# Six head pairs of the attention's last product as one unit, with the last 64 keys in four 64x64 tiles

## The chip, the cores and the metric

The kernel runs on one core of one Trainium2 chip. The metric is the device time of one execution in microseconds (us), lower is better. The engines are named as in the profile: PE (TensorE matmuls), PEld (TensorE weight loads), DVE (VectorE), ACT (ScalarE), POOL (GpSimd) and SP (SyncE, which only issues DMAs here).

## The reference

The kernel computes an attention layer that mixes its heads before and after the softmax, and two dense layers behind it. The change lies in the attention alone:

```python
def _attn_ref(q, k, v, w_pre, w_post):           # q, k, v: 4 batches, 12 heads, 448 tokens, 64 wide
    scale = 1.0 / np.sqrt(q.shape[-1])
    scores = scale * np.matmul(q, k.transpose(0, 1, 3, 2))
    scores = np.einsum('bhij,hg->bgij', scores, w_pre)
    scores = scores - np.max(scores, axis=-1, keepdims=True)
    attn = np.exp(scores)
    attn = attn / (np.sum(attn, axis=-1, keepdims=True) + 1e-09)
    attn = np.einsum('bhij,hg->bgij', attn, w_post)
    return np.matmul(attn, v).astype(np.float32)  # "AV" below

def reference(...):
    x = attn_out.transpose(0, 2, 1, 3).reshape(B * S, H * D)
    x = _moe_ref(x=x, **moe_kwargs)               # x @ w_in, softmax-weighted, layer norm, @ w_out
    return _moe2_ref(x=x, **moe2_kwargs)          # relu(x @ w_in)^2 @ w_out
```

## The kernel before, in words

The queries of a batch are cut into chunks of 120, 120, 120 and 88 tokens, 16 chunks in all, numbered c = 0 to 15. A chunk is cut into blocks of up to 10 tokens times 12 heads, and two blocks make a slot: slots s = 0 to 89 follow one another in one loop, and the order in which that loop writes its instructions is the order in which each engine runs them. In one slot the loop writes

- the loads that fall due (K, V, Q, and pieces of the first dense layer's weights), the DMAs of K, V and the weight pieces on POOL's queue, and on SP's queue the DMAs that lay scores out anew for slot s + 5 (`shuffle`);
- `pre(s + 2)`: the head mix before the softmax, on PE, into its own four banks;
- `post_out(s - 1)`: two DVE copies that take the result of the head mix after the softmax out of PSUM;
- `qk`: scores of one pair of heads of a later chunk, on PE, taken out by ACT (six per chunk, so most slots have one, a few have two or none);
- `negmax` on DVE and `expo` on ACT for slot s + 2;
- `av`, where a chunk is complete, taken out of PSUM by ACT;
- `weigh(s + 1)` on POOL: three small instructions that make the matrix w, which `post(s + 1)` multiplies by;
- the work on weight pieces (below), and at the end `post(s)` on PE, which needs w of `weigh(s)`.

`qk`, `av` and `post` take their PSUM from one ring of two buffers of two banks each (`ring()`, L132).

AV of a chunk is 6 pairs of heads times 448 keys. The keys come as three tiles of 128 and a rest of 64. V of the rest lies in a tile with zeros (`load_v`, L176): for one head of a pair its 64 keys stand in partitions 0 to 63 and zeros below, for the other the reverse, so that the rest, too, is a product over 128 partitions. A unit `av(c, a)` handles three pairs: for each, four key tiles times two heads, each head in its own half of the output's partitions. Its 24 products of 128 x 64 by 128 x 120 (or by 88) write one bank, and ACT copies that bank out. A chunk has two units, three slots apart (L544: `end + 1 + 3 * a`).

The 48 weight pieces of the first dense layer (`w1pieces`) run beside this: a DMA loads a piece (POOL's queue, at most 7 pieces ahead), ACT squares it, DVE makes three passes over it, POOL makes two (`flush`: L96 and L97), ACT scales it, and SP stores it. The passes of DVE are handed out one at a time by `filler()`: seven in a slot that has a unit of AV, none elsewhere (L610). At most four pieces are between start and flush (L601). In a slot POOL flushes whatever pieces DVE has finished by then, behind the `weigh` of that slot. Once the last piece is stored, `prep_first` loads and splits the weights of the dense layer (POOL: L441), most of it from slot 80 on.

The lines that the change and the prediction touch: `load_v` L176, `post` L277, `av` L319, `flush` L95, `weigh` L261, `narrow_w1` L385, the slot of AV L544, the limit on pieces L601, the passes handed out L610.

Of the kernel before, what the change touches and what calls it, by code (L numbers as in the profile page):

```python
# [7 lines left out]
F32 = mybir.dt.float32  # L8
# [10 lines left out]
def kernel(  # L19
# [23 lines left out]
    R = 10  # L43
# [133 lines left out]
    def load_v(b, j):  # L177
        if j < NJ:
            t = late_p.tile([JW, H, D], F32, tag=f"v_{j}", name="v", bufs=2)
            nc.gpsimd.dma_start(out=t, in_=v[b, j * JW:(j + 1) * JW].rearrange("j (g d) -> j g d", g=H))  # L180
        else:
            t = late_p.tile([128, 2, G2, D], F32, tag=f"v_{j}", name="v", bufs=2)
            src = v[b, j * JW:S].rearrange("j (e g d) -> e j g d", e=2, g=G2)
            for e in range(2):
                nc.gpsimd.memset(t[64 - 64 * e:128 - 64 * e, e], 0.0)
            for e in range(2):
                nc.gpsimd.dma_start(out=t[64 * e:64 * e + 64, e], in_=src[e])
        vv[b, j] = t

    def qk(c, p, dve=0):  # L190
# [88 lines left out]
    def post(s):  # L279

        ps = ring()
        w = ws.pop(s)
        for b in range(2):
            e = es.pop((s, b))
            for j in range(NJ + 1):
                for x in range(2):
                    for u in range(2):
                        c = x ^ u
                        m = H * size(2 * s + b, u ^ b)
                        o = j * JW + c * 64 if j < NJ else NJ * JW  # L290
                        g0, ng = (0, H) if j < NJ else (c * G2, G2)
                        i0 = (b * NU + j * H) * RH
                        nc.tensor.matmul(  # L293
                            out=ps[64 * c:64 * c + 64, u, i0:i0 + ng * RH],
                            lhsT=e[64 * u:64 * u + m, o:o + 64],
                            rhs=w[64 * u:64 * u + m, b, g0:g0 + ng],
                            start=True,
                            stop=True,
                        )
        pps[s] = ps  # L300
# [15 lines left out]
                m, o = size(2 * s + b, g), oa + RH * g  # L316
                nc.vector.tensor_copy(at[c][:, :, o:o + m], pv[:, b, :, 0:m])

    def av(c, a):  # L319

        ch = chunks[c]
        n = ch["n"]
        if c not in xt:
            xt[c] = late_p.tile([128, HP, 120], F32, tag="xt", name="xt", bufs=2)
        ps = ring()
        for q in range(3):
            p = 3 * a + q
            for j in range(NJ + 1):
                t = vv[ch["b"], j]
                for e in range(2):  # L330
                    g = p + e * HP
                    nc.tensor.matmul(  # L332
                        out=ps[64 * e:64 * e + 64, 0, q * 120:q * 120 + n],
                        lhsT=t[:, g] if j < NJ else t[:, e, p],
                        rhs=at[c][:, j * H + (g if j < NJ else p), 0:n],
                        start=(j == 0),
                        stop=(j == NJ),
                    )

        pv = ps[:, 0, 0:360].rearrange("p (q t) -> p q t", q=3)  # L340
        x = xt[c][:, 3 * a:3 * a + 3]
        if n == 120:
            nc.scalar.copy(
                x.rearrange("p q (u i k) -> p q u k i", u=2, i=R),
                pv.rearrange("p q (u k i) -> p q u k i", u=2, i=R),
            )
        else:
            for u, m in enumerate((ch["n0"], n - ch["n0"])):
                nk = -(-m // R)
                kf = m - (R - 1) * nk  # L350
                for k0, k1, i1 in ((0, kf, R), (kf, nk, R - 1)):
                    if k0 < k1:
                        o, z = u * ch["n0"], k0 * R + u * ch["n0"]
                        nc.scalar.copy(
                            x[:, :, o:o + i1 * nk].rearrange("p q (i k) -> p q k i", k=nk)[:, :, k0:k1],
                            pv[:, :, z:z + (k1 - k0) * i1].rearrange("p q (k i) -> p q k i", i=i1),
                        )
        if a == 1:
            at.pop(c)

    def x_out(c, eng=nc.sync):
        ch = chunks[c]
# [21 lines left out]

    def narrow_w1(i):  # L385
        src, dst, k, o = w1pieces[i]
        sq = raw_p.tile([128, WP], F32, tag="w1sq", name="w1sq", bufs=4)
        t = raw_p.tile([128, WP], F32, tag="w1t", name="w1t", bufs=7)
        for step, _ in enumerate(narrow(w1raw.pop(i), sq, t, nc.gpsimd)):
            if step == 3:  # L390
# [77 lines left out]
        nc.sync.dma_start(out=g_sb, in_=g_ln.rearrange("(k p) -> p k", p=128))  # L468


    wz = raw_p.tile([128, 256], F32, tag="w1sq", name="wz", bufs=4)
    nc.gpsimd.memset(wz, 0.0)
    wz = wz.bitcast(mybir.dt.bfloat16)[:, 0:448]

# [64 lines left out]
    for c, ch in enumerate(chunks):  # L539
# [1 line left out]
            for j in range(NJ + 1):  # L541
                at_slot((ch["first"] + 1) // 2 + (3 if c == 0 else 0) + j, load_v, ch["b"], j)
        end = (ch["first"] + ch["nb"] + 1) // 2
        for a in range(2):  # L544
            at_slot(min(end + 1 + 3 * a, NP), av, c, a)
        at_slot(min(end + 6, NP), x_out, c)
    last_qk = max(s for s, js in jobs.items() for f, a in js if f is qk)
    w1at = []
    kept = 0
# [8 lines left out]
    for s in range(lo_s, NP + 2):  # L558
# [39 lines left out]
                f(*a)  # L598
        if 0 <= s + 1 < NP:
            weigh(s + 1)  # L600
        while begun < len(w1at) and w1at[begun] <= s - 3 and len(fill) + len(w1f) < 4:  # L601
            start_w1(begun)
            begun += 1
        for i in scales:
            scale_w1(i)
        for i in sorted(w1f):
            sq, t = w1f.pop(i)
            flush(sq, t)
            w1s[i] = t
        for _ in range(7 if any(f is av for f, a in js) else 0):  # L610
            filler()
        if 0 <= s < NP:
            post(s)
# [421 lines left out]
```

## Time and profile before

| what | us |
|---|---|
| median of the runs shown (lowest to highest of 3) | 1128.45 (1126.77 to 1129.98) |
| the profiled execution: its time, its span | 1130.63, 1128.8 |
| PE busy, share of the span | 1068.8, 95% |
| DVE, ACT, POOL busy | 680.3 (60%), 468.3 (41%), 417.8 (37%) |
| AV's matmuls (L332): busy, first and last start | 82.2, from 56.8 to 411.1 |

The attention fills the first 411 us or so; behind it the dense layers keep PE busy without gaps. The shares over the whole span hide what happens in the attention, where POOL, DVE and ACT carry far more than on the average. A matmul of this kernel is in fp32, and stands in the trace as two PE matmuls and two weight loads: "x48" of L332 is one unit of 24 products.

### The profile page before, as it was taken

What the parts mean: (1) busy time and instruction counts of PE and PEld (TensorE: products, weight loads), DVE (VectorE), ACT (ScalarE), POOL (GpSimd) and SP (SyncE); (2) the same over time, 40 slices, a digit from 0 to 9 for tenths busy, and PEclk for the clock granted to TensorE, in tenths of its full rate; (3) what the DMA queues carried; (4) which work ended last, traced back from release to release, by engine and by line L of the source; (5) the groups of instructions that cost most, each with busy time, mean ns of one, the idle gap of its engine ahead of it and who ended that gap; (6) DMA issues with size and microseconds to landing.
All of it is one profiled execution on the core that took longest, in us unless ns stands there. A gap on an engine that the chain in (4) does not pass through costs nothing.

```text
span 1128.8 us, 30803 instructions
## 1 busy us (share of the span) xinstructions
PE 1068.8 (95%) x12920; PEld 925.7 (82%) x12920; DVE 680.3 (60%) x1201; ACT 468.3 (41%) x1026; POOL 417.8 (37%) x642
## 2 busy tenths in 40 slices
PE   7798987987999899999999999999999999999998
PEld 2464654655656688989989999999999999999998
DVE  2555875765785638534434686366666666766734
ACT  4465765665876624221212466322222322323211
POOL 2464897787694837201110553011111111111100
PEclk9898999998999999999999999999999999999999
DMA  5786778778776624111110654011211121111113
GB/s 154 193 217 208 215 240 248 208 229 232 217 222 189 186 86 127 50 49 57 35 36 21 197 182 124 24 57 56 57 57 56 43 60 53 57 56 56 30 71 126
DMA packets 96715, 135.00 MB, mean 120 GB/s; under 512 B 21728, under 2 KB 81376, under 8 KB 96576
## 3 DMA queue, kind: packets, MB, share of 16 engines
q1 hardware_dynamic: 88640, 110.16, 32.5%
q0 software_dynamic: 6336, 22.22, 6.9%
q8 instruction: 102, 1.67, 0.6%
q10 hardware_dynamic: 1600, 0.64, 0.2%
q14 instruction: 37, 0.30, 0.1%
HBM read 71.65 MB, written 22.81 MB: 84 GB/s over the span
## 4 chain that ended last, share of the span: by engine, by line
PE 86%; issue 4%; POOL 3%; DMA 3%; ACT 2%; DVE 1%; SPq 1%; POOLq 0%; ACTq 0%; DVEq 0%
PE ps_h L899 21%; PE ps_y L938 21%; PE ps_o L745 10%; PE ps_h L453 10%; PE ps_ring L293 7%; PE ps_ring L332 6%; PE ps_pre L236 5%; PE ps_ring L202 5%; DMA sdst<-ssrc 2%; PE ps_tr L731 1%; ACT ssrc L209 1%; POOL sm L265 1%; ACT e L254 1%; POOL w1sq L96 0%; POOL w1t L97 0%
## 5 line engine op out<-in xcount | busy, mean ns | idle before, releaser
L899 PE MATMUL ps_h<-x,ti 128*128 128x384 f32 (+1 forms) x1440 | 241.6, 325 | 0.0
L938 PE MATMUL ps_y<-to,g 128*128 128x384 f32 x1332 | 240.0, 337 | 0.0
L899 PEld LDWEIGHTS ps_h<-x,ti 128*128 128x128 f32 x1440 | 236.5, 188 | 0.0
L938 PEld LDWEIGHTS ps_y<-to,g 128*128 128x128 f32 x1332 | 232.2, 188 | 1.7 <-DVE y L949 1.7
L293 PEld LDWEIGHTS ps_ring<-w,e 60*64 60x64 f32 (+1 forms) x5760 | 105.0, 140 | 75.8 <-issue 46.2
L312 DVE COPY at<-ps_ring 128x420 f32<-128x420 f32 x156 | 87.8, 611 | 110.5 <-PE ps_ring L293 110.5
L293 PE MATMUL ps_ring<-w,e 60*64 60x60 f32 (+2 forms) x5760 | 113.3, 225 | 34.6 <-issue 26.6
L209 ACT COPY ssrc<-ps_ring 128x896 f32<-128x896 f32 x93 | 83.3, 906 | 111.7 <-PE ps_ring L202 99.9
L907 ACT ACTIVATE r<-ps_h 128x384 f32<-128x384 f32 (+1 forms) x80 | 37.5, 469 | 215.7 <-PE ps_h L899 215.7
L453 PE MATMUL ps_h<-w1i,xs 128*128 128x512 f32 x504 | 122.1, 400 | 0.0
L745 PE MATMUL ps_o<-zt,w1o 128*128 128x384 f32 (+1 forms) x720 | 119.9, 326 | 0.0
L254 ACT ACTIVATE e<-ps_pre,nm 128x448 f32<-128x448 f32 x180 | 113.0, 638 | 16.0 <-DVE nm L247 13.3
L908 DVE SCALAR_TENSOR_TENSOR r<-ps_h,r 128x384 f32<-128x384 f32 (+1 forms) x80 | 42.4, 531 | 123.7 <-ACT r L907 123.7
L745 PEld LDWEIGHTS ps_o<-zt,w1o 128*128 128x128 f32 x720 | 116.8, 189 | 0.0
L453 PEld LDWEIGHTS ps_h<-w1i,xs 128*128 128x128 f32 x504 | 95.5, 191 | 21.8
L949 DVE TENSOR_TENSOR y<-ps_y,y 128x768 f32<-128x768 f32 x97 | 92.4, 953 | 31.5 <-PE ps_y L938 31.5
L855 POOL TENSOR_TENSOR ti<-wt,ti 128x384 fp32r<-128x384 f32 x32 | 35.1, 1095 | 205.8 <-ACT ti L854 205.8
L247 DVE TENSOR_REDUCE nm<-ps_pre 128x1 f32<-128x448 f32 x180 | 103.3, 612 | 13.1 <-PE ps_pre L236 12.8
L202 PE MATMUL ps_ring<-k,q 64*64 64x448 f32 x768 | 102.2, 563 | 6.0 <-issue 2.1
L236 PE MATMUL ps_pre<-sdst,wpre_bd 64*64 64x448 f32 x720 | 101.0, 578 | 6.3 <-DMA sdst<-ssrc 3.9
L332 PEld LDWEIGHTS ps_ring<-at,v 128*64 128x64 f32 x1536 | 75.1, 138 | 29.8 <-PE ps_pre L236 12.7
L332 PE MATMUL ps_ring<-at,v 128*64 128x120 f32 (+1 forms) x1536 | 82.2, 263 | 7.5 <-issue 5.4
(84 smaller groups left out, 1183.0 us busy)
## 6 DMA issues: line engine op xcount, KB each, us to landing
sdst<-ssrc SPq DMA_DIRECT2D x172, 210.0 KB
wr<-in_moe_w_in_dram SPq DMA_DIRECT2D x32, 384.0 KB
wr<-in_moe_w_out_dram SPq DMA_DIRECT2D x32, 384.0 KB
w1raw<-in_moe_w_in_dram POOLq DMA_DIRECT2D x24, 256.0 KB, 5.9
w1raw<-in_moe_w_out_dram POOLq DMA_DIRECT2D x24, 256.0 KB, 5.1
out_dram<-y SPq DMA_DIRECT2D x13, 384.0 KB
v<-in_v_dram POOLq DMA_DIRECT2D x12, 384.0 KB, 6.3
xraw<-xD SPq DMA_DIRECT2D x12, 384.0 KB
```

Source lines behind the costliest of these rows:

```text
L202: nc.tensor.matmul(out=ps[64 * u:64 * u + 64, e, 0:S], lhsT=qq[c][64 * e:64 * e + 64, p * n + u * half:p * n + u * half + 64], rhs=k[64 * ...
L209: (nc.vector.tensor_copy if dve else nc.scalar.copy)(ssrc[c][:, p:H:HP, :], ps[:, :, 0:S])
L236: nc.tensor.matmul(out=ps[b][64 * u:64 * u + 64, 0:S], lhsT=wpre_bd[64 * r:64 * r + m], rhs=ds[b][64 * r:64 * r + m], start=True, stop=True,)
L247: nc.vector.tensor_reduce(out=nm, in_=pres[s][b][:, 0:S], op=ALU.max, axis=AX.X, negate=True)
L254: nc.scalar.activation(out=e, in_=pres[s][b][:, 0:S], func=AF.Exp, bias=nms.pop((s, b)), scale=1.0, accum_out=sms[s][:, b:b + 1])
L293: nc.tensor.matmul(out=ps[64 * c:64 * c + 64, u, i0:i0 + ng * RH], lhsT=e[64 * u:64 * u + m, o:o + 64], rhs=w[64 * u:64 * u + m, b, g0:g0 ...
L332: nc.tensor.matmul(out=ps[64 * e:64 * e + 64, 0, q * 120:q * 120 + n], lhsT=t[:, g] if j < NJ else t[:, e, p], rhs=at[c][:, j * H + (g if ...
L453: nc.tensor.matmul(out=ps[:, u], lhsT=t[:, a, cc], rhs=w1i[cc][:, w, u * 512:(u + 1) * 512], start=(cc == 0 and a == 0 and w == 0), stop=( ...
L745: nc.tensor.matmul(out=ps[:, 0:width], lhsT=w1o[k][:, w, cc * 128:(cc + 1) * 128], rhs=zT[:, a, k, 0:width], start=(k == 0 and i == 0), st ...
L899: nc.tensor.matmul(out=ps[:, 0:n], lhsT=ti[:, w, cc, f * 128:(f + 1) * 128], rhs=x2[q][:, a, cc], start=(cc == 0 and i == 0), stop=(cc == ...
L938: nc.tensor.matmul(out=ps[:, u - us[0], 0:DM // 2], lhsT=g[:, a, f, o:o + 128], rhs=to[:, w, f, u * (DM // 2):(u + 1) * (DM // 2)], start= ...
L949: nc.vector.tensor_tensor(out=yo, in0=po, in1=yo, op=ALU.add)
```

## The change

A chunk's AV becomes one unit, `av(c)`, in the slot of the former first half. It uses both banks of one ring buffer: three pairs in each. First come the 36 products over the three full key tiles, then the rest: its V lies in half the space, without zeros, one half of the heads in partitions 0 to 63 and the other half in 64 to 127, and each of the 12 products is 64 x 64 by 64 x 120. Four consecutive ones use four different quarters of the array. `post` writes the last 64 keys of the heads into the partition halves that fit this (the moving operand takes two groups of three heads instead of six in a row). ACT takes the two banks out one after the other. `x_out` comes three slots earlier.

The handing out of the weight pieces changes with it: twelve DVE passes in a slot with AV, one in every odd slot without; up to six pieces between start and flush, with six buffers for the squares instead of four.

```diff
@@ load_v
-            t = late_p.tile([128, 2, G2, D], F32, tag=f"v_{j}", name="v", bufs=2)
-            src = v[b, j * JW:S].rearrange("j (e g d) -> e j g d", e=2, g=G2)
-            for e in range(2):
-                nc.gpsimd.memset(t[64 - 64 * e:128 - 64 * e, e], 0.0)
-            for e in range(2):
-                nc.gpsimd.dma_start(out=t[64 * e:64 * e + 64, e], in_=src[e])
+            t = late_p.tile([128, G2, D], F32, tag=f"v_{j}", name="v", bufs=2)
+            src = v[b, j * JW:S].rearrange("j (a n d) -> j a n d", a=4, d=D)
+            nc.gpsimd.dma_start(out=t[0:64].rearrange("j (a n) d -> j a n d", a=2), in_=src[:, 0:4:3])
+            nc.gpsimd.dma_start(out=t[64:128].rearrange("j (a n) d -> j a n d", a=2), in_=src[:, 1:3])
@@ post
+                        wb = w[64 * u:64 * u + m, b]
+                        if j == NJ:
+                            wb = wb.rearrange("p (a n) i -> p a n i", a=4)
+                            wb = wb[:, 1:3] if c else wb[:, 0:4:3]
...
-                            rhs=w[64 * u:64 * u + m, b, g0:g0 + ng],
+                            rhs=wb,
@@ av
-    def av(c, a):
+    def av(c):
...
+        def product(p, e, half, j):
+            t = vv[ch["b"], j]
+            a, q = divmod(p, 3)
+            rows = slice(0, 128) if half is None else slice(64 * half, 64 * half + 64)
+            g = p + e * HP if half is None else (p + 3 * half) % HP
+            nc.tensor.matmul(
+                out=ps[64 * e:64 * e + 64, a, q * 120:q * 120 + n],
+                lhsT=t[rows, g],
+                rhs=at[c][rows, j * H + g, 0:n],
+                start=(j == 0 and q == 0),
+                stop=(j == NJ and q == 2),
+            )
+
+        for p in range(HP):
+            for j in range(NJ):
+                for e in range(2):
+                    product(p, e, None, j)
         for q in range(3):
...
+            for a in range(2):
                 for e in range(2):
...
+                    product(3 * a + q, e, a ^ e, NJ)
+
+        for a in range(2):
+            pv = ps[:, a, 0:360].rearrange("p (q t) -> p q t", q=3)
...
@@ narrow_w1
-        sq = raw_p.tile([128, WP], F32, tag="w1sq", name="w1sq", bufs=4)
+        sq = raw_p.tile([128, WP], F32, tag="w1sq", name="w1sq", bufs=6)
@@ the slots
-        for a in range(2):
-            at_slot(min(end + 1 + 3 * a, NP), av, c, a)
-        at_slot(min(end + 6, NP), x_out, c)
+        at_slot(min(end + 1, NP), av, c)
+        at_slot(min(end + 3, NP), x_out, c)
@@ the loop over slots
-        while begun < len(w1at) and w1at[begun] <= s - 3 and len(fill) + len(w1f) < 4:
+        while begun < len(w1at) and w1at[begun] <= s - 3 and len(fill) + len(w1f) < 6:
...
-        for _ in range(7 if any(f is av for f, a in js) else 0):
+        for _ in range(12 if any(f is av for f, a in js) else s % 2):
             filler()
```

PE around the AV of chunk 10, slots 64 to 67: L332 is a unit of AV, L293 `post`, L236 `pre`, L202 `qk`. Before, from the first unit to the second:

```order
L332 MATMUL ps_ring<-at,v 64x120 x24
L293 MATMUL ps_ring<-w,e 64x60 x12
...
L202 MATMUL ps_ring<-k,q 64x448 x4
L293 MATMUL ps_ring<-w,e 64x60 x12
...
L202 MATMUL ps_ring<-k,q 64x448 x4
L293 MATMUL ps_ring<-w,e 64x60 x12
...
L202 MATMUL ps_ring<-k,q 64x448 x4
L332 MATMUL ps_ring<-at,v 64x120 x24
```

The same place now (L333 is AV, L295 `post`, L200 `qk`):

```order
L333 MATMUL ps_ring<-at,v 64x120 x48
L295 MATMUL ps_ring<-w,e 64x60 x12
...
L200 MATMUL ps_ring<-k,q 64x448 x4
L295 MATMUL ps_ring<-w,e 64x60 x12
...
L200 MATMUL ps_ring<-k,q 64x448 x4
L295 MATMUL ps_ring<-w,e 64x60 x12
...
L200 MATMUL ps_ring<-k,q 64x448 x4
L295 MATMUL ps_ring<-w,e 64x60 x12
```

The second unit has moved in front, into the first, and the slot three later has no AV.

POOL at the same place: L267 ends `weigh(66)`, L96 and L97 flush a piece, L264 begins `weigh(67)`. Before:

```order
L267 TENSOR_TENSOR w<-wpost_bd,sm 128x120
L96 TENSOR_SCALAR w1sq<-w1sq 128x256
L97 TENSOR_TENSOR w1t<-w1t,w1sq 128x256
L96 TENSOR_SCALAR w1sq<-w1sq 128x256
L97 TENSOR_TENSOR w1t<-w1t,w1sq 128x256
L96 TENSOR_SCALAR w1sq<-w1sq 128x256
L97 TENSOR_TENSOR w1t<-w1t,w1sq 128x256
L264 TENSOR_SCALAR sm<-sm 128x2
```

Now (L265 ends `weigh(66)`, L262 begins `weigh(67)`):

```order
L265 TENSOR_TENSOR w<-wpost_bd,sm 128x120
L96 TENSOR_SCALAR w1sq<-w1sq 128x256
L97 TENSOR_TENSOR w1t<-w1t,w1sq 128x256
L96 TENSOR_SCALAR w1sq<-w1sq 128x256
L97 TENSOR_TENSOR w1t<-w1t,w1sq 128x256
L96 TENSOR_SCALAR w1sq<-w1sq 128x256
L97 TENSOR_TENSOR w1t<-w1t,w1sq 128x256
L96 TENSOR_SCALAR w1sq<-w1sq 128x256
L97 TENSOR_TENSOR w1t<-w1t,w1sq 128x256
L262 TENSOR_SCALAR sm<-sm 128x2
```

Four pieces are flushed between the two `weigh`, where there were three. From chunk 2 to chunk 11 every slot behind an AV now flushes four pieces in a row; before, a slot behind a unit flushed two or three, and there were twice as many such slots.

## Rows read from the trace of the kernel before

**Rows 1.** The page: busy time by engine, and the chain that ended last.
```profile
PE 1068.8 (95%) x12920; PEld 925.7 (82%) x12920; DVE 680.3 (60%) x1201; ACT 468.3 (41%) x1026; POOL 417.8 (37%) x642
PE 86%; issue 4%; POOL 3%; DMA 3%; ACT 2%; DVE 1%; SPq 1%; POOLq 0%; ACTq 0%; DVEq 0%
```

**Rows 2.** Windows: stretch, length, busy time (instructions) by engine, PEclk, DMA share, GB/s.
```profile
110.00:343.00 233.00, 205.83 (x5458) 139.93 (x5454) 167.83 (x367) 157.94 (x378) 186.53 (x333) 0.97 0.76 225
```

**Rows 3.** Timeline of PE: start, us, line, operation, count, idle before.
```profile
305.72 0.96 PE L202 MATMUL ps_ring<-k,q 64*64 64x448 f32 x8
306.61 2.68 PE L332 MATMUL ps_ring<-at,v 128*64 128x120 f32 x48
309.22 1.13 PE L293 MATMUL ps_ring<-w,e 60*64 60x60 f32 x64
310.18 0.96 PE L236 MATMUL ps_pre<-sdst,wpre_bd 64*64 64x448 f32 x8
310.96 0.93 PE L202 MATMUL ps_ring<-k,q 64*64 64x448 f32 x8
311.71 1.11 PE L293 MATMUL ps_ring<-w,e 60*64 60x60 f32 x64
314.15 1.12 PE L293 MATMUL ps_ring<-w,e 60*64 60x60 f32 x64
```

**Rows 4.** Timeline of POOL, the same stretch.
```profile
309.83 0.40 POOL L264 TENSOR_SCALAR sm<-sm 128x2 f32<-128x2 f32 x1 [1.19 <-ACT e L254]
311.58 0.86 POOL L96 TENSOR_SCALAR w1sq<-w1sq 128x256 f32<-128x256 f32 x1
312.52 0.73 POOL L97 TENSOR_TENSOR w1t<-w1t,w1sq 128x256 f32<-128x256 f32 x1
...
316.01 0.73 POOL L97 TENSOR_TENSOR w1t<-w1t,w1sq 128x256 f32<-128x256 f32 x1
316.82 0.22 POOL L264 TENSOR_SCALAR sm<-sm 128x2 f32<-128x2 f32 x1
317.92 0.56 POOL L267 TENSOR_TENSOR w<-wpost_bd,sm 128x120 f32<-128x120 f32 x1
```

**Rows 5.** The chain in order of time, end of the attention: start, us, what.
```profile
395.41 1.13 PE ps_ring L293 x64
405.08 6.25 PE ps_ring L332 x144
411.33 2.96 PE ps_h L453 x12
```

**Rows 6.** Groups of instructions: busy us, mean ns of one, idle before.
```profile
L343 ACT COPY xt<-ps_ring 128x360 f32<-128x360 f32 x24 | 19.8, 823 | 20.8 <-PE ps_ring L332 20.8
L354 ACT COPY xt<-ps_ring 128x150 f32<-128x150 f32 (+2 forms) x24 | 5.3, 376 | 4.1 <-PE ps_ring L332 4.1
L87 DVE SCALAR_TENSOR_TENSOR w1t<-w1raw,w1t 128x256 uint32<-128x256 uint32 x48 | 21.9, 457 | 1.4
L83 DVE SCALAR_TENSOR_TENSOR w1t<-w1raw,w1t 128x256 uint32<-128x256 uint32 x48 | 20.6, 430 | 1.4
L79 DVE TENSOR_SCALAR w1t<-w1raw 128x256 uint32<-128x256 uint32 x48 | 14.7, 306 | 0.1
L382 POOL DMA_DIRECT2D w1raw<-in_moe_w_out_dram x24 | 14.2, 594 | 6.6 <-DVE w1t L79 6.5
```

**Rows 7.** Waits in 110 to 343: who for whom, us, times, longest us.
```profile
PE ps_ring L293 <- issue: 16.6, 12, 3.0
PE ps_ring L332 <- issue: 3.4, 2, 1.8
PE ps_ring L202 <- issue: 2.1, 2, 1.5
PE ps_ring L293 <- POOL w L267: 2.0, 3, 1.1
```

**Rows 8.** A gap of PE on its timeline, and the window behind it.
```profile
194.63 0.71 PE L293 MATMUL ps_ring<-w,e 60*64 60x30 f32 x34 [2.56 <-issue]
195.50:198.90 3.40, 3.40 (x24) 1.62 (x18) 3.22 (x8) 0.62 (x1) 0.40 (x1) 0.50 0.34 113
```

**Rows 9.** Window near the end of the attention, columns as in rows 2.
```profile
392.00:397.00 5.00, 2.10 (x102) 1.91 (x95) 1.54 (x3) 3.53 (x9) 4.75 (x7) 0.99 0.57 160
```

More of the change, by code (lines that the diff above doesn't have):

```diff
@@ L290, in post @@
                         o = j * JW + c * 64 if j < NJ else NJ * JW
-                        g0, ng = (0, H) if j < NJ else (c * G2, G2)
                         i0 = (b * NU + j * H) * RH
+                        ng = H if j < NJ else G2
+                        wb = w[64 * u:64 * u + m, b]
+                        if j == NJ:
+                            wb = wb.rearrange("p (a n) i -> p a n i", a=4)
+                            wb = wb[:, 1:3] if c else wb[:, 0:4:3]
                         nc.tensor.matmul(
@@ L317, in post_out @@
                 nc.vector.tensor_copy(at[c][:, :, o:o + m], pv[:, b, :, 0:m])
-    def av(c, a):
+    def av(c):
         ch = chunks[c]
         n = ch["n"]
-        if c not in xt:
-            xt[c] = late_p.tile([128, HP, 120], F32, tag="xt", name="xt", bufs=2)
+        xt[c] = late_p.tile([128, HP, 120], F32, tag="xt", name="xt", bufs=2)
         ps = ring()
+        def product(p, e, half, j):
[14 more added lines that the diff above has]
+                    product(p, e, None, j)
@@ L326, in av @@
         for q in range(3):
-            p = 3 * a + q
-            for j in range(NJ + 1):
-                t = vv[ch["b"], j]
+            for a in range(2):
                 for e in range(2):
[L331 to L347, printed above, removed]
+                    product(3 * a + q, e, a ^ e, NJ)
+        for a in range(2):
+            pv = ps[:, a, 0:360].rearrange("p (q t) -> p q t", q=3)
+            x = xt[c][:, 3 * a:3 * a + 3]
+            if n == 120:
+                nc.scalar.copy(
+                    x.rearrange("p q (u i k) -> p q u k i", u=2, i=R),
+                    pv.rearrange("p q (u k i) -> p q u k i", u=2, i=R),
+                )
+                continue
@@ L357, in av @@
                         )
-        if a == 1:
-            at.pop(c)
+        at.pop(c)
     def x_out(c, eng=nc.sync):
@@ L468, in load_const @@
         nc.sync.dma_start(out=g_sb, in_=g_ln.rearrange("(k p) -> p k", p=128))
-    wz = raw_p.tile([128, 256], F32, tag="w1sq", name="wz", bufs=4)
+    wz = raw_p.tile([128, 256], F32, tag="w1sq", name="wz", bufs=6)
     nc.gpsimd.memset(wz, 0.0)
```

## The prediction

> **What bounds the kernel now.** I read the page's shares and chain first [rows 1]: PE is busy 95% of the span and carries 86% of the chain, so over the whole it looks like a kernel that only PE bounds. The windows say otherwise for the attention [rows 2]: from 110 to 343 us, where the weight pieces run beside it, PE is busy 205.8 of 233 us, but POOL 186.5 (80%), and DVE 167.8 (72%). The timeline shows the beat there [rows 3]: from one `post` to the next 2.49 us (309.22 to 311.71) and 2.44 us in slots with one qk, PE without a gap; a slot with a unit of AV takes 2.7 more. POOL's timeline of the same stretch [rows 4] shows the other bound: it waits for the exponentials until 309.83, makes w for slot 66, flushes three pieces from 311.58 to 316.82, and only then begins w for slot 67. The waits [rows 7] tell what PE loses in that stage: 16.6 + 3.4 + 2.1 = 22.1 us to "issue" (its instructions were late), and so far only 2.0 us to POOL.
>
> **The change part by part.** *Products.* A unit's 24 products take 2.68 us [rows 3]; the two heads of a pair run side by side in the two column halves, so 12 steps of 0.223 us. The new unit has 18 such steps, 4.02 us, and 12 products of a quarter of the array. If four of them run together, that is three steps; the trace has no such step of 120 columns. Its bounds: qk runs four quarters at 448 columns in 0.75 us (310.96 to 311.71), so 120 columns take at least 0.20; and if they only pair up, six steps of 0.223, 1.34 in all. I take 0.22 a step, near qk's row, which has the same tiles: 0.66. Unit 4.68 us against 5.36: 0.68 less. The 88-wide chunks: the last 144 matmuls, 6.25 us [rows 5], are one unit of 120 and two of 88, so (6.25 - 2.68) / 2 = 1.785 each; new 2.68 + 3 x 0.16 = 3.16 against 3.57: 0.41 less. Twelve chunks and four: 12 x 0.68 + 4 x 0.41 = 9.8 us of PE's time (ends 0 and 10.7).
>
> That the quarters do run together rests on pre: it issues its four quarters in the new unit's pattern, two neighbours in different row halves writing the two partition halves of one bank, and takes 0.78 us (310.18 to 310.96), as long as qk, whose row halves have a bank each [rows 3]. The Trainium skill, "TensorEngine Tiling (Array Packing)", section "Gotcha 1: PSUM Pressure", says that different row tiles cannot access the same PSUM bank at once. By that rule the first and second product of each four would wait for each other and the gain of 9.8 would fall to about 0; by pre's row it stays. The trace disagrees with the rule here; it is a rival below.
>
> *Taking the unit out.* Two copies of 0.82 us follow AV instead of one [rows 6], 1.65. The ring buffer is wanted again by the next slot's qk, post and pre later: 0.96 + 0.78 = 1.74 us [rows 3]. Hidden. In 88-wide chunks six copies of 0.376, 2.26 us: 0.5 late in four chunks, if not hidden 2.0; I take 0.5 in all.
>
> *DVE.* A piece is 0.31 + 0.43 + 0.46 = 1.2 us of DVE [rows 6]. Twelve passes are 4.8 us, beside an AV of 4.68; seven were 2.8 beside 2.68. The odd single pass (0.4) lies in DVE's idle time of 28%. I cost both at nothing; if the cover failed, post's copies would come 0.1 to 0.4 us later in some slots. The memsets that go from POOL are two for each batch, the split DMA issues stay four: nothing.
>
> *POOL.* This is the wait that I expect to be late next. A flush takes (316.82 - 311.58) / 3 = 1.75 us a piece, and four in a row 7.0. Take chunk 10, whose order is shown, with times of rows 3 and 4. AV would end at 306.61 + 4.68 = 311.29, and `post` of slots 64, 65, 66, 67 be ready to start about 311.2, 313.7, 316.15 and 318.6. POOL begins to flush at 311.58 as now, ends at 318.6, and has w for slot 67 1.6 us later: 320.2. PE waits 1.6 us. Before, slot 67 held the second unit, so its `post` was not wanted before about 320.3: that unit was POOL's cover, and it has gone to the front. Behind the waiting `post` PE has the whole next slot queued (pre, qk), and DVE's and ACT's copies wait for those; SP's shuffles run five slots ahead and don't care. The other nine flushes of four differ by the DMA issues that POOL has to make before that `weigh` (0 to 3 of 0.59 us [rows 6]), by 1.5 us less AV in 88-wide chunks, and by 0.75 where one of the three slots has two qk or none. Counted so, place by place (chunks 2 to 11): 2.7, 4.0, 2.6, 0.3, 2.4, 4.0, 3.5, 0, 1.6, 2.8, together 23.9 us if PE lost nothing else. But PE loses 22.1 us to "issue" in about 53 slots [rows 7], 0.42 a slot, 1.25 in the three slots in question, and that time hides as much of POOL's. Left: 1.45, 2.75, 1.35, 0, 1.15, 2.75, 2.25, 0, 0.35, 1.55 = 13.6 us. Ends: 0 and 23.9. POOL's 2.0 us of now [rows 7] are of this kind and go.
>
> *Clock.* A long gap of PE has a price behind it: after one of 2.56 us the granted clock was 0.50, 1.2 GHz, for 3.4 us, in which PE does half the work [rows 8]; 1.7 us lost. I take three of the eight gaps: 5 us. Ends: 0 and 8 x 1.7 = 13.6.
>
> *The end.* The last stretch before the dense layer is AV of 6.25 us [rows 5]; it becomes one 88-wide unit, 3.16, since chunk 14's second half goes to slot 87. There PE idles (busy 2.10 of 5 us, POOL 4.75 [rows 9]), so this is a gain of 3.1, while the faster products of chunks 13 and 14 gain nothing beside POOL. Against the 0.68 + 0.68 + 0.41 counted above that is 1.3 more. The pieces end three slots sooner, and the first split of POOL's next job moves out of this POOL-bound end: I take 1.0 (ends 0 and 1.8).
>
> *Sum.* -9.8 - 1.3 - 1.0 - 2.0 + 0.5 + 13.6 + 5 = +5.0 us against the profiled execution, whose span is 1128.8 and time 1130.63. That execution lies 2.2 above the median, so the time I predict is 1128.45 + 5 = 1133 us.
>
> **The rivals.** *A: POOL's burst stays hidden, faster.* PE's gain comes through: -9.8 - 1.3 - 1.0 - 2.0 = -14.1, 1114 us; with a third of the waits, 1119. For it: three flushes in a row cost PE only 2.0 us so far [rows 7], and late instructions may fall just where POOL would have been late. Against it: the worked example has no slack left. It decides if w comes earlier than 1.25 us after PE wants it in most of the ten places. *B: the waits show in full and each gap is followed by half clock.* -14.1 + 23.9 + 13.6 + 0.5 = +23.9, 1152 us. For it: 80% load of POOL, with bursts; against it: PE's own losses always cover some. *C: the bank rule holds and the quarters run in pairs.* The unit costs as before, so +5.0 + 9.8 = +14.8, 1143 us. Against it: pre's row. *D: the change moves where PE's late instructions fall;* those 22.1 us come in about a dozen and a half gaps, and a few more or fewer make 5 us either way.
>
> **How the numbers follow.** Forecast, from about -1 to +12 around 1133: 0.40 (of it faster 0.04, same 0.14, slower 0.22). A 0.32 (faster 0.28, same 0.04). B 0.16 and C 0.04, slower. D around no change, 0.08 (0.03, 0.02, 0.03). A measurement of this kernel tells about 0.3%, 3.4 us, from no change. Faster 0.35, same 0.20, slower 0.45. The range of 8 in 10 takes in A's 1114 and stops short of B's end: 1114 to 1147. The forecast's own range is 1127 to 1140.
>
> **What would show it.** The step of `post` after an AV slot stays 2.49, the AV unit itself reads about 4.7 us (5.4 would be C). In the slot three behind an AV, `post` has an idle of 1 to 3 us put down to POOL's w in most of chunks 2 to 11, and the waits of PE on POOL rise from 2.0 to some 14 us in that stage. POOL shows eight flush instructions in a row without a gap. The end of the attention has 3 us less AV. I am wrong if those idles are missing (then A), or if PE's "issue" waits change by more than the POOL waits do (then D).

## The result

Over 20 runs of each the changed kernel takes 1133.93 us in the median (1126.11 to 1143.56), the kernel before 1128.41 (1118.31 to 1138.25). The ratio is 1.0057, 95% interval 1.0035 to 1.0079: slower by 0.57%. The profiled execution of the changed kernel took 1140.57 us, 6.6 above its median, that of before 2.2 above its own; so the two traces differ by 9.9 us where the medians differ by 5.5, and what the traces show is larger than what is to be explained.

### The profile page after: what moved, and what is told of

Same layout as the page of the kernel before. It is cut to its first block, busy times and chain, and to the rows that moved or that the text cites. A ratio compares the mean times of both kernels' runs of the same rounds, so it can differ in the third digit from the quotient of the medians.

```text
span 1138.8 us, 30832 instructions
## 1 busy us (share of the span) xinstructions
PE 1064.3 (93%) x12920; PEld 922.3 (81%) x12920; DVE 680.5 (60%) x1201; ACT 467.1 (41%) x1026; POOL 415.1 (36%) x634
## 4 chain that ended last, share of the span: by engine, by line
PE 82%; POOL 7%; DMA 4%; issue 3%; ACT 2%; SPq 1%; DVE 0%; POOLq 0%; ACTq 0%; DVEq 0%
PE ps_h L908 21%; PE ps_y L947 21%; PE ps_h L463 10%; PE ps_o L754 10%; PE ps_ring L295 5%; PE ps_pre L234 5%; PE ps_ring L200 4%; PE ps_ring L333 4%; DMA sdst<-ssrc 3%; POOL w1sq L96 2%; POOL w1t L97 2%; ACT ssrc L207 1%; POOL sm L263 1%; PE ps_tr L740 1%; SPq L214 1%
## 5 line engine op out<-in xcount | busy, mean ns | idle before, releaser
L295 PEld LDWEIGHTS ps_ring<-w,e 60*64 60x64 f32 (+1 forms) x5760 | 108.5, 141 | 85.7 <-POOL w L265 39.0
L295 PE MATMUL ps_ring<-w,e 60*64 60x60 f32 (+2 forms) x5760 | 113.2, 225 | 41.2 <-POOL w L265 23.3
L234 PE MATMUL ps_pre<-sdst,wpre_bd 64*64 64x448 f32 x720 | 105.2, 597 | 11.1 <-issue 7.4
L200 PE MATMUL ps_ring<-k,q 64*64 64x448 f32 x768 | 103.2, 570 | 5.9 <-ACT ssrc L207 2.4
L333 PEld LDWEIGHTS ps_ring<-at,v 128*64 128x64 f32 (+1 forms) x1536 | 69.6, 142 | 25.2 <-ACT ssrc L207 16.2
L333 PE MATMUL ps_ring<-at,v 128*64 128x120 f32 (+3 forms) x1536 | 75.6, 271 | 10.8 <-ACT ssrc L207 10.3
```

Source lines behind the costliest of these rows:

```text
L200: nc.tensor.matmul(out=ps[64 * u:64 * u + 64, e, 0:S], lhsT=qq[c][64 * e:64 * e + 64, p * n + u * half:p * n + u * half + 64], rhs=k[64 * ...
L234: nc.tensor.matmul(out=ps[b][64 * u:64 * u + 64, 0:S], lhsT=wpre_bd[64 * r:64 * r + m], rhs=ds[b][64 * r:64 * r + m], start=True, stop=True,)
L295: nc.tensor.matmul(out=ps[64 * c:64 * c + 64, u, i0:i0 + ng * RH], lhsT=e[64 * u:64 * u + m, o:o + 64], rhs=wb, start=True, stop=True,)
L333: nc.tensor.matmul(out=ps[64 * e:64 * e + 64, a, q * 120:q * 120 + n], lhsT=t[rows, g], rhs=at[c][rows, j * H + g, 0:n], start=(j == 0 and ...
```

## The profile after

The page, answering to [rows 1]: the chain gives PE 4 points less and POOL 4 points more.

```profile
PE 1064.3 (93%) x12920; PEld 922.3 (81%) x12920; DVE 680.5 (60%) x1201; ACT 467.1 (41%) x1026; POOL 415.1 (36%) x634
PE 82%; POOL 7%; DMA 4%; issue 3%; ACT 2%; SPq 1%; DVE 0%; POOLq 0%; ACTq 0%; DVEq 0%
```

Nearly all of the loss lies in one stretch, from the first `post` to that of slot 81, the last before the tail of the attention (1.2 us more pass ahead of it). Its window in the kernel before, columns as in [rows 2]:

```profile
26.00:372.65 346.65, 301.83 (x7808) 204.20 (x7800) 230.36 (x489) 222.47 (x526) 245.11 (x448) 0.96 0.75 217
```

and in the changed kernel, with the stretch of [rows 2] behind it:

```profile
27.24:386.83 359.59, 300.26 (x7850) 204.86 (x7852) 229.90 (x489) 221.70 (x527) 244.26 (x443) 0.93 0.73 211
110.00:343.00 233.00, 192.09 (x4976) 129.69 (x4972) 158.85 (x348) 143.90 (x347) 179.09 (x313) 0.93 0.76 221
```

The stretch is 12.9 us longer: PE is busy 1.6 us less and idle 14.5 us more, and its granted clock fell from 0.96 to 0.93. What follows is shorter: from slot 81 to the dense layer 38.6 us before and 34.6 now. The timeline of PE, around slots 19 to 22 and at slots 36, 58 and the last AV, shows the things that the prediction spoke of:

```profile
104.33 4.69 PE L333 MATMUL ps_ring<-at,v 128*64 128x120 f32 x96
...
111.45 1.08 PE L295 MATMUL ps_ring<-w,e 60*64 60x60 f32 x64
...
113.89 1.10 PE L295 MATMUL ps_ring<-w,e 60*64 60x60 f32 x64
...
119.54 1.93 PE L295 MATMUL ps_ring<-w,e 60*64 60x60 f32 x64 [3.00 <-POOL w L265]
121.27 1.75 PE L234 MATMUL ps_pre<-sdst,wpre_bd 64*64 64x448 f32 x8
...
180.50 0.90 PE L234 MATMUL ps_pre<-sdst,wpre_bd 60*64 60x448 f32 x1 [3.95 <-issue]
...
280.26 1.82 PE L200 MATMUL ps_ring<-k,q 64*64 64x448 f32 x16
286.70 6.13 PE L333 MATMUL ps_ring<-at,v 128*64 128x120 f32 x96 [4.62 <-ACT ssrc L207]
...
417.94 3.57 PE L333 MATMUL ps_ring<-at,v 128*64 128x88 f32 x96
421.43 3.92 PE L463 MATMUL ps_h<-w1i,xs 128*128 128x512 f32 x16
```

The new unit reads 4.69 us, two units of 2.68 before [rows 3]. `post` follows `post` by 2.44 us. In the third slot behind the AV it waits 3.00 us for w, and `pre` and `post` then take nearly twice their time. POOL's timeline of that place, answering to [rows 4], has eight flush instructions in a row between w for slot 21 and w for slot 22, the third behind the AV:

```profile
109.18 0.59 POOL L265 TENSOR_TENSOR w<-wpost_bd,sm 128x120 f32<-128x120 f32 x1
109.85 0.86 POOL L96 TENSOR_SCALAR w1sq<-w1sq 128x256 f32<-128x256 f32 x1
110.79 0.73 POOL L97 TENSOR_TENSOR w1t<-w1t,w1sq 128x256 f32<-128x256 f32 x1
...
115.09 0.90 POOL L96 TENSOR_SCALAR w1sq<-w1sq 128x256 f32<-128x256 f32 x1
116.08 0.73 POOL L97 TENSOR_TENSOR w1t<-w1t,w1sq 128x256 f32<-128x256 f32 x1
116.75 1.17 POOL L392 DMA_DIRECT2D w1raw<-in_moe_w_in_dram  x2
118.00 0.22 POOL L262 TENSOR_SCALAR sm<-sm 128x2 f32<-128x2 f32 x1
118.30 0.72 POOL L263 TENSOR_TENSOR sm<-sm,eps_sb 128x2 f32<-128x2 f32 x1
119.10 0.39 POOL L265 TENSOR_TENSOR w<-wpost_bd,sm 128x120 f32<-128x120 f32 x1
```

The window behind that wait has the granted clock at its lower level (0.50, 1.2 GHz) for 6.83 us; the second window, behind the wait at 286.70, for 3.41:

```profile
119.05:125.88 6.83, 6.34 (x144) 4.46 (x148) 3.71 (x9) 1.99 (x6) 6.13 (x13) 0.50 0.86 277
286.30:289.71 3.41, 3.00 (x30) 3.01 (x32) 0.00 (x0) 2.40 (x6) 0.83 (x2) 0.50 0.65 227
```

The waits of PE in the long stretch, the largest of the changed kernel:

```profile
PE ps_ring L295 <- POOL w L265: 17.2, 8, 3.8
PE ps_ring L295 <- issue: 14.3, 12, 4.3
PE ps_ring L333 <- ACT ssrc L207: 10.3, 6, 4.6
PE ps_pre L234 <- issue: 7.4, 3, 3.9
...
ACT ssrc L207 <- DMA sdst<-ssrc: 18.8, 5, 4.7
```

and the same lines of the kernel before:

```profile
PE ps_ring L293 <- issue: 26.6, 19, 4.3
PE ps_ring L332 <- issue: 5.4, 3, 2.0
...
PE ps_ring L332 <- ACT ssrc L209: 2.1, 5, 0.9
PE ps_ring L293 <- POOL w L267: 2.0, 3, 1.1
...
ACT ssrc L209 <- DMA sdst<-ssrc: 9.0, 3, 4.6
```

PE's waits on POOL rose from 2.0 to 17.6 us here. In the window of [rows 7], from 110 to 343, they rose from 2.0 to 15.6, where some 14 were forecast; their main line there:

```profile
PE ps_ring L295 <- POOL w L265: 15.2, 6, 3.8
```

A second wait, not forecast, rose by 8: AV waits for ScalarE's copy of a QK into `ssrc`. The rows at 280.26 and 286.70 show how. In a slot with two QKs the AV needs the ring buffer of the first; ScalarE copies that buffer only when the shuffles of the chunk two earlier have left `ssrc`, and here they are late. What SP, which issues them, does at this place:

```profile
269.87 4.31 SPq L418 DMA_DIRECT2D w1oD<-w1t  x4
274.27 1.20 SPq L174 DMA_DIRECT2D q<-in_qT_dram  x2
275.56 12.59 SPq L214 DMA_DIRECT2D sdst<-ssrc  x10
```

Ten shuffles stand behind weight stores and take 1.26 us each, in slots that want two every 2.49 us; the median shuffle of the long stretch holds SP for 0.83 us, single ones in this row for up to 2.3. ScalarE's copy starts at 285.75 after waiting 4.68 us for them.

A third line moved that was not to move: "issue", time for which the profile shows no wait, 35.1 us of PE in the stretch before and 24.2 now. The DMA part of the page shows, before and after alike, the transfers that load instructions (number, MB, share):

```profile
q8 instruction: 102, 1.67, 0.6%
```

That is one transfer of 16384 bytes for every 253 of PE's 25840 matmuls and weight loads. Of the 42 gaps put down to "issue" in the two stretches, 41 end 2.2 to 3.0 us after the start of such a transfer, the one at 180.50 in slot 36 for example 2.4 us after. In the 14 traces of this document it is 276 of 284, though the times that lie so far behind a transfer make up only 14% of the stretch. So these gaps are, as far as traces can tell, PE waiting for its own instructions. No run here changes how they are loaded.

## The experiments

A table first, since the same reading recurs: the ratio to before, and from the trace of each the idle time of PE from the first `post` to that of slot 81 (the waits summed by the engine that ended them; small ones left out), with ScalarE's wait for shuffles in the same stretch. The traces are single executions: they lie between 6.8 us below the median of their kernel (e1) and 6.6 above it (changed; e8 6.2 above), so a difference of a few us between two of them is weak evidence. In e3 11.9 us put down to DVE stand in no column.

```
kernel                         ratio   95%               PE idle  POOL  ACT   issue  ACT for shuffles
before                         1                          44.7     2.0   6.1  35.1    9.0
changed                        1.0057  1.0035 to 1.0079   58.8    17.6  16.0  24.2   18.8
e1 one flush a slot            1.0052  1.0019 to 1.0086   57.3    12.7  18.5  21.6   29.5
e2 x stored two slots later    1.0124  1.0086 to 1.0163   67.8    12.6  15.3  38.2   29.0
e3 both                        1.0117  1.0070 to 1.0165   67.3     4.5  22.0  27.1   26.9
e4 one unit, old rest          1.0087  1.0052 to 1.0123   57.8    15.6  11.0  30.6   22.8
e5 no flush, changed           1.0146  1.0109 to 1.0182   63.4     0.7  27.2  34.1   30.2
e6 no flush, before            1.0029  1.0000 to 1.0057   42.9     0.7   9.5  29.9   12.9
e7 AV one slot later           1.0122  1.0091 to 1.0153   50.7    17.6  12.5  17.5   18.3
e8 shorter weigh               1.0064  1.0032 to 1.0097   63.2     7.5  20.8  33.8   37.3
e9 stores on ScalarE's queue   1.0112  1.0067 to 1.0158   60.7     5.9  29.8  23.4   30.0
e10 the same, before           1.0145  1.0096 to 1.0194   57.4     1.9  17.3  36.7   16.4
e11 no flush and e9            1.0121  1.0083 to 1.0158    66.6   1.5  39.8   23.9   30.7
e12 double QKs at the end      1.0033  1.0007 to 1.0059   53.5     8.2  13.9  28.4   18.4
```

The first theory was the prediction's: the burst of flushes costs what the products gain (theory 1). Its rival, from the trace after: SP's order, with the store of x waiting for ScalarE at end + 3, makes the shuffles late (theory 2).

**One flush a slot (e1).**

```
-        for i in sorted(w1f):
+        for i in sorted(w1f)[:1]:
```

> The changed kernel, but POOL flushes at most one weight piece in a slot, so the four that DVE finishes behind an AV are spread over four slots; all else, AV included, stays. Theory 1 (POOL's burst of four flushes, 7 us, holds up w for the slot three behind an AV, whose cover of 2.7 us of AV has gone): the waits of PE's post on POOL's w between 110 and 350 us fall from 16.6 us to under 5, and the time from 1134 to about 1120 us, 0.5 to 1.2% under the kernel before. Rival, theory 2 (the shuffles on SP's queue come late, because the store of AV's result now waits for a longer AV, and the scores' buffer comes free late, so that AV waits for ACT and ACT for a DMA): the waits of PE on POOL may fall, but the AV's waits on ACT (10.3 us) stay, and the time stays at 1130 to 1135.

Ratio 1.0052: nothing came back. PE's longest wait on w fell from 3.8 to 1.7 us, but there are 11 in place of 8, 12.7 us in all, and ScalarE's wait for the shuffles rose to 29.5. The profiled execution was one of the faster, 1131.16 against a median of 1137.99, so its trace shows this kernel at its better.

**The store of x two slots later (e2), and both (e3).**

```
-        at_slot(min(end + 3, NP), x_out, c)
+        at_slot(min(end + 5, NP), x_out, c)
```

> The changed kernel, but the store of a chunk's AV result stands two slots later in SP's queue; all else stays. Theory 2: SP's idle of 2 to 6 us before each such store goes, the shuffles behind it come sooner, the waits of AV on ACT's copy of the scores fall from 10.3 us to about 3, and the time falls by 4 to 8 us, to 1126 to 1130. Theory 1: SP's idles go, but nothing on PE's path changes but a little; 1131 to 1135 us, and the waits of post on POOL's w stay at 14 to 19 us.

> Both edits together: one flush a slot, and the store two slots later. If both waits are on PE's path and apart, the two gains add: 1112 to 1120 us, about 1% under the kernel before. By theory 1 alone it is as the first edit alone (about 1120), by theory 2 alone as the second alone (1126 to 1130).

Both came out the other way, 1.0124 and 1.0117. SP's waits at the store of x did go (40.4 us in the changed kernel, 0.9 in e2, summed over line 376), but those at the weight stores rose from 37.7 to 54.5 and ScalarE's for the shuffles from 18.8 to 29.0. Theory 2 in this form fell: the store of x is not what makes the shuffles late.

**One unit with the old rest (e4).** The last 64 keys again in 128 rows with zero halves, everything else as in the changed kernel.

```
-        for q in range(3):
-            for a in range(2):
-                for e in range(2):
-                    product(3 * a + q, e, a ^ e, NJ)
+            for j in range(NJ + 1):
+                ...
+                        lhsT=t[:, g] if j < NJ else t[:, e, p],
+                        rhs=at[c][:, j * H + (g if j < NJ else p), 0:n],
```

> The changed kernel with the last 64 keys as before: V with zeros and products over 128 partitions, so the AV unit has 48 products in 24 steps, 5.36 us instead of 4.6; the one unit, its slot, the handing out of passes and the flushes stay as changed. Theory 1: 0.7 us more of AV in each chunk is 0.7 us more cover for the burst, so the waits on POOL's w fall by some 5 us while AV's own time rises by 10; 1135 to 1140 us, 0.6 to 1.1% over the kernel before. A rival that the quarter products are what slows the kernel (bank conflicts, more semaphore waits): the time falls to 1128 or under.

Its unit, on its timeline:

```profile
104.55 5.14 PE L333 MATMUL ps_ring<-at,v 128*64 128x120 f32 x96
109.62 0.57 PE L294 MATMUL ps_ring<-w,e 60*64 60x60 f32 x24
```

From the unit's start to `post` that is 5.07 us, against 104.33 to 108.83, 4.51 (the trace's next row), with the quarter tiles and 2 x 2.61 before. With the 88-wide chunks (3.79, 3.39 and 2 x 1.97) the quarters take 12 x 0.56 + 4 x 0.40 = 8.3 us off PE; the ratio to before moved by 0.0030, 3.4 us, with overlapping intervals. So the quarter tiles are not what slows the kernel, the rival of this run. One unit in one slot with the old products is slower than before by 0.9%, and that is shown; but the new handing out of the weight pieces (twelve passes, six pieces) is in this kernel too, and no run takes the two apart.

**No flush (e5 of the changed kernel, e6 of the kernel before).** The two instructions of the flush are left out, so small weights are not set to zero.

```
         for i in sorted(w1f):
             sq, t = w1f.pop(i)
-            flush(sq, t)
             w1s[i] = t
```

> The changed kernel without GpSimd's flush of the narrowed weight pieces (lines 96 and 97 of the changed kernel: small values are not set to zero; 2 instructions and some 1.65 us of GpSimd for each of 48 pieces). Everything else stays, the six pieces in flight and the conversion bursts too. Theory 1 (the burst of flushes behind an AV slot holds the weighting back, and PE with it): PE's waits on w fall from 17 us to under 3, the idles three slots behind an AV are gone, the time falls by 12 to 17 us to about 1119, ratio to before 0.985 to 0.992. Theory 2 (what ate the gain is the AV unit behind the first QK's copy in slots with two QKs, where that copy waits for the shuffles): the waits on w fall, but the idles before AV at slots 13, 36, 58 and 75 stay or grow, and the time falls by under 6 us, ratio 1.000 to 1.005.

> The kernel before without the same flush (lines 96 and 97): the baseline of the run without flush of the changed kernel. Theory 1: PE waited for w only 2 us in before, so the time falls by 1 to 4 us (ratio 0.996 to 0.999), and the changed kernel without flush stands 5 to 10 us below this one. Theory 2: this one falls as much as the changed one does, and the two keep their distance of 4 to 7 us. A third theory, GpSimd as a bound of the whole attention part in both kernels: both fall by over 10 us.

This is the run on which theory 1 fell. The burst is gone and with it PE's waits on w, and the kernel is slower than with it, 1.0146. The waits of PE in e5:

```profile
PE ps_ring L295 <- issue: 25.2, 18, 3.4
PE ps_ring L333 <- ACT ssrc L207: 17.5, 7, 5.7
PE ps_pre L234 <- issue: 5.0, 3, 2.7
```

Against the changed kernel PE's waits on POOL fell by 16.9 us, those on ScalarE rose by 11.2, AV's wait for the copy first among them, and those put down to "issue", for PE's instructions, by 9.9. Theory 2 had the waits right and the time wrong: it put the ratio at 1.000 to 1.005. In the kernel before the same cut moved nothing that can be told, 1.0029, so the third theory, GpSimd as the bound of both, fell too. Without any flush the change costs 1.2% by these ratios, more than the 0.57% with it.

**AV one slot later (e7).**

```
-        at_slot(min(end + 1, NP), av, c)
-        at_slot(min(end + 3, NP), x_out, c)
+        at_slot(min(end + 2, NP), av, c)
+        at_slot(min(end + 4, NP), x_out, c)
```

> The changed kernel with the AV unit at end + 2 in place of end + 1 and the store of x at end + 4: no AV stands any more in a slot with two QKs (slots 13, 36, 58 and 75 before). Theory 2: the idles of 2.2, 4.0, 4.6 and 2.8 us before those AVs and the cold stretches behind them go, the time falls by 8 to 14 us, to 1120 to 1126 and a ratio of 0.992 to 0.998. Theory 1: the bursts move by one slot with the AV and cost the same, time within 3 us of the changed kernel, ratio 1.003 to 1.008.

AV's waits for ScalarE are gone from this trace, yet the median is 1139.68, ratio 1.0122. Part of that lies in the tail: from slot 82 to the dense layer it takes 36.9 us, the changed kernel 32.8. PE is idle about as long in both (6.4 and 6.1 us); the granted clock is 0.86 there against 1.00, and PE busy 30.5 us against 26.7. The profiled execution was the fastest of the seven, so where its median loses the rest stays open.

**A shorter weighting (e8).** The addition of 1e-9 to sums that are at least 1 is left out, which changes no bit.

```
-        nc.gpsimd.tensor_scalar(out=sm, in0=sm, scalar1=1e-9, scalar2=None, op0=ALU.add)
```

> The changed kernel without the addition of 1e-9 to the sums of the softmax (line 262; each sum holds exp(0) = 1 and is at least 1, where the addition changes no bit of a float32). One GpSimd instruction of 0.22 us and the gap behind it, about 0.3 us, go in each of 90 slots from the chain that ends in w. Theory 1: each of the some seven waits behind a burst gets 0.3 us shorter, 2 us in all, ratio 1.002 to 1.006. Theory 2: no change. The third theory (GpSimd bounds the whole part): 0.3 us a slot over 75 slots, the time falls by 10 to 20 us.

PE's waits on POOL fell from 17.6 to 7.5 us, ScalarE's for the shuffles doubled to 37.3; the ratio is 1.0064. As in e5 the gain is lost elsewhere, by a cut that leaves the burst in place: PE's waits on ScalarE rose by 4.8 us and those for its instructions by 9.6.

**The stores on ScalarE's queue (e9; e10 in the kernel before; e11 with no flush besides).** In e11 small weights are not set to zero.

```
-    def x_out(c, eng=nc.sync):
+    def x_out(c, eng=nc.scalar):
...
-        nc.sync.dma_start(out=dst[k * 128:(k + 1) * 128, o:o + WP], in_=w1t.pop(i))
+        nc.scalar.dma_start(out=dst[k * 128:(k + 1) * 128, o:o + WP], in_=w1t.pop(i))
```

> The changed kernel with the two stores that wait for ScalarE, x (line 376) and the narrowed weight pieces (line 418), issued by ScalarE's own queue in place of SP's. Nothing is left out; the same bytes move. Removing the flush made the changed kernel slower and moved the loss to the QK copy that waits for the shuffles, so the theory now (call it 2b) is that SP, which issues the shuffles in order behind stores that wait for ScalarE, is late in the five slots without AV: SP's waits of 28 us for x and some 25 us for pieces go, the shuffles leave earlier, the idles before AV at slots 13, 36, 58 and 75 fall under 1.5 us and the time by 8 to 14 us, ratio 0.992 to 0.998. Theory 4 (the DMA engines themselves are full, 75% busy): the shuffles land no earlier, time within 3 us of the changed kernel, ratio 1.003 to 1.008. Against both: ScalarE has 0.66 us for each issue, some 90 of them, 60 us on an engine that is busy 62% of this part; if that decides, the time rises by 5 to 10 us.

> The kernel before with the same two stores on ScalarE's queue: the baseline of the run of the changed kernel. Theory 2b: before has an AV half every third slot, in which SP catches up, so it gains little, 0 to 4 us, ratio 0.996 to 1.000, and the changed kernel with these queues comes out 3 to 8 us below it. Theory 4: no change here either, and the changed kernel stays 4 to 7 us above. ScalarE's time decides: both rise by the same.

> The changed kernel with both taken away: GpSimd's flush left out (lines 96 and 97, small values are not set to zero) and the stores on ScalarE's queue. If the burst of flushes and the order of SP's queue are two limits of nearly the same height, so that taking one away only shows the other, this one falls by more than the two single runs together: 1115 to 1120, ratio 0.985 to 0.992. If the shuffles' own transport is the limit (theory 4), it stays at the 1142 us of the run without flush alone, ratio 1.008 to 1.015.

All three are slower, 1.0112, 1.0145 and 1.0121, and the kernel before loses most: 76 issues moved to an engine that PE already waits for cost more than they did on SP's queue. The expectation had this case (5 to 10 us more if ScalarE's time decides), but not that the kernel before would lose more than the changed one. e11 came where theory 4 put it, and the joint gain of two limits did not come. In e9 the shuffles had SP nearly to themselves, and ScalarE's copies still waited for them:

```profile
ACT ssrc L207 <- DMA sdst<-ssrc: 30.0, 6, 6.7
```

That speaks against SP's order as the only cause. It does not yet speak for the shuffles' transport alone: SP waited 200.8 us at the shuffles themselves (89.2 in the changed kernel), 62.8 of it for ScalarE and 83 for `qk` and `pre` on PE, so the shuffles also start late because what they read or overwrite is late. Since ScalarE has the stores besides, the causes are not told apart. Between e9 and e10, both with ScalarE loaded, the change costs nothing that can be told (1.0112 against 1.0145, overlapping).

**Double QKs at the end of their stretch (e12).**

```
-                s = beg + p * (end - beg) // HP
+                s = end - 1 - (HP - 1 - p) * (end - beg) // HP
```

> The changed kernel with the QKs of a chunk placed from the end of their stretch (slot end - 1 - (5 - p) * (end - beg) // 6 in place of beg + p * (end - beg) // 6): a slot with two QKs is then never an AV slot, and the same six QKs lie in the same slots otherwise. In the changed kernel the seven AV slots with two QKs have PE idle 2.15, 0.28, 1.20, 3.95, 4.62, 0.28 and 3.14 us, 15.6 us in all, the other AV slots 1.5 us in all; there the AV needs the PSUM buffer that the first QK's copy holds, and the copy waits for the shuffles to land. Theory 2: with one QK the AV takes the other buffer and covers that wait, those idles fall under 4 us in all and the time by 8 to 14 us, ratio 0.992 to 0.999. Theory 5, from the runs so far (several limits of nearly one height, so that what one place gives back is lost at the next): the idles there go, others grow, the time stays within 5 us of the changed kernel, ratio 1.002 to 1.010.

No AV slot has two QKs now. Its largest waits of PE:

```profile
PE ps_ring L295 <- issue: 21.0, 14, 3.4
PE ps_ring L295 <- ACT ssrc L207: 8.4, 9, 2.1
PE ps_ring L295 <- POOL w L265: 7.4, 8, 2.1
PE ps_ring L333 <- issue: 3.2, 2, 2.5
```

The line of AV behind `ssrc` (10.3 us in the changed kernel) is gone; `post`, one step later, waits for `ssrc` 8.4 us in place of 2.7. Idle is 53.5 us, the lowest of the kernels whose unit stands at end + 1, and the ratio 1.0033, the lowest of all kernels with one unit and still above 1. Against the changed kernel's 1.0057 the intervals overlap, so a gain over it is not shown. Of the idles that the expectation counts as waits for the shuffles, the 3.95 us at slot 36 are put down to "issue", a wait for PE's instructions. The timeline of slot 36 shows a unit without a wait ahead of it, and its last 24 matmuls, the quarters, as a row of their own (the second is the end of the first):

```profile
178.03 4.69 PE L333 MATMUL ps_ring<-at,v 128*64 128x120 f32 x96
...
181.88 0.85 PE L333 MATMUL ps_ring<-at,v 64*64 64x120 f32 x24
182.54 1.09 PE L295 MATMUL ps_ring<-w,e 60*64 60x60 f32 x64
```

Theory 5 is what stands, by elimination: several limits of nearly one height. In the traces of the changed kernel, e1, e4, e5 and e8, which leave every QK, AV and store in its slot, PE is idle 57 to 63 us, whichever cause is cut; in the kernel before, with or without flush, 43 to 45. One of the limits is the loading of PE's instructions, at which no run aims. Take "issue" off PE's idle time in the table, and the same kernels have 34.6, 35.7, 27.2, 29.3 and 29.4 us left, the kernel before 9.6. In these traces, then, leaving out the flush took 5.3 us from the other waits, and the waits for instructions grew by 9.9; single traces can't say whether the one follows from the other. No run takes two of the limits away cleanly: the later store of e3 did not free SP, and e11 loads ScalarE. No version tried beats the kernel before.

## Why the prediction was right in its number and wrong in its account

- *Products, -9.8.* Right. From unit to `post` 4.51 us against 2 x 2.61, and 3.39 against 2 x 1.97: 12 x 0.71 + 4 x 0.55 = 10.7 us. The 88-wide unit before had been read too short, 1.785 us. The quarters' part was put at 0.66 us; from 181.88 to 182.54 it takes 0.66.
- *Rival C, the bank rule.* The trace has a unit of 4.69 us, where C had the quarters in pairs and a unit of about 5.4. The Trainium skill, "TensorEngine Tiling (Array Packing)", section "Gotcha 1: PSUM Pressure", says that different row tiles cannot access the same PSUM bank at once; the trace disagrees with the rule here, and the measurement decides.
- *POOL, +13.6 and -2.0.* Right as a reading: PE's waits on POOL are 17.6 us against 2.0, mostly in the slot named, after eight flushes in a row. It is so in six of the ten places (slots 22, 33, 45, 55, 67 and 72); the two dearest of the forecast, 2.75 us each in slots 27 and 49 behind 88-wide units, show no such wait, so that the sum fits is in part luck. Wrong as a price: with the flushes left out the time does not fall by it, it rises by 0.9% (e5 against the changed kernel).
- *The step that failed* is the sentence "SP's shuffles run five slots ahead and don't care". They run ahead of `pre`, which reads them, but the next QK copy into the same `ssrc` buffer comes one slot behind the last of them. ScalarE waits for the shuffles 18.8 us in place of 9.0, and PE for ScalarE 16.0 in place of 6.1. A likely reason, not tested by itself, is that two units three slots apart had given SP and the DMAs time to catch up, where now five slots of 2.5 us follow each other. What POOL's side gives back ends in this wait and in PE's waits for its instructions (e5, e8).
- *Taking the unit out, +0.5, and DVE, nothing.* Right: PE waits 0.6 us for the copies into `xt` and 0.7 for DVE's.
- *Clock, +5.* Right. The units before slot 81 took 6.8 us less (11 of 4.51 and 3 of 3.39 against 21 of 2.61 and 6 of 1.97), PE's busy time fell by 1.6 only, so about 5.2 went to the lower clock, 0.93 against 0.96: 47.8 us of the stretch are at 0.50, 30.7 before.
- *The end, -1.3, and the preparation, -1.0.* With the unit gains counted elsewhere in that stretch about -4.1 was forecast for it; 38.6 became 34.6. Not all of it is for the reasons given: from slot 82 on the granted clock is 1.00 in place of 0.95, which no term had, and POOL is busy 24.7 us in place of 24.6, so the preparation's gain is not seen.
- *Rival D, PE's late instructions.* They changed by -10.9 us (35.1 to 24.2), the forecast of no change was wrong by that. It is about what the ScalarE wait added (+9.9), and so the two unforeseen terms cancelled in the sum: in this the number is luck. The sign that was to show D, a change larger than that of the POOL waits (+15.6), did not come.
- *Rivals A and B, the burst hidden or in full.* Neither came true: the waits on POOL are 17.6 us, where B had 23.9, and e1 shows that even a burst spread thin doesn't lead to A.

So +5.0 was forecast and +5.5 measured between the medians, with the place of one wait right, its price not, and two missed terms of opposite sign. Still open: whether the shuffles are late by SP's order, by their transport or by their inputs (e9 changed ScalarE too); what the new handing out of the weight pieces does by itself; what sets the length of PE's waits for its instructions; and why the kernel without the flush is slower than the changed one and not the same.

## What to carry to other kernels

Where four engines are each busy some 60% of a stretch or more, a wait in the trace names the limit that ended last there, not what its removal gives: price it only after asking which wait stands behind it, and test it by taking the cause away. Work of the bound engine that lies in two portions may also be a pause for every queue that runs ahead; making one portion of it saves the engine's time and can take the pause away (here argued, not shown). Gaps in which an engine waits for nothing that the profile shows are worth comparing with the transfers that load instructions. When a buffer is reused, follow it in both directions: a transfer that is far ahead of its reader may be just in time for the next writer.

## What the runs showed of the hardware

- Two row halves of the array that write neighbouring partition halves of one PSUM bank run side by side: the unit's 24 quarter matmuls of 120 columns take 0.66 us from first to the next `post` (e12), where six pairs at 0.223 us would take 1.34.
- A DMA issue on ScalarE's queue holds ScalarE for 0.72 us in the mean in e9 and 0.65 in e10; 76 issues moved there made the kernel before 1.45% slower (e10).
- PE's gaps put down to "issue" go with the loading of its instructions: 276 of 284 in the 14 traces end 2.2 to 3.0 us after the start of a 16384-byte transfer of the instruction queue. Their sum differs widely, 35.1 us before, 24.2 in the changed kernel, 38.2 in e2, with the same number of PE instructions (12920 of each kind before and after).
